# Block-sparse attention into top-1 experts: probabilities as the stationary operand, denominators and gate logits taken from the same matmul, bounds with queries stationary

## The chip, the cores and the metric

The kernel runs on one core of one Trainium2 chip, written in Bass with the Tile scheduler. The metric is the time of one execution on the device in microseconds. The engines are PE (TensorE), DVE (VectorE), ACT (ScalarE), POOL (GpSimd) and SP (SyncE, which here only issues transfers).

## The reference

Attention over 4 batches of 8 heads, 768 tokens, head size 64, in fp32, and then a mixture of 8 experts with one expert per token:

```python
ub = sum(maximum(q * k_min[chunk], q * k_max[chunk]))   # bound per query and chunk of 32 keys
sel = the 6 chunks with the largest ub among the causal ones
scores = q @ k.T / 8, kept where sel and causal, else -1e9
attn = softmax(scores) @ v                               # 3072 tokens x 512
expert = argmax(attn @ w_gate); gate = softmax(attn @ w_gate)[expert]
out = gate * (relu(attn @ w1[expert]) @ w2[expert])      # 512 -> 1024 -> 512
```

## The kernel before

**Pairs.** Two heads make a pair, so there are 16 pairs (`i`), four per batch (`hp` = 0 to 3 within batch `b`). A pair's work is cut into seven units `u` by the causal triangle: a query half `qb` of 384 tokens against key blocks of 128. Units 0 and 1 belong to the first half, 2 to 6 to the second; units 1 and 6 hold two narrower parts (256 and 128 queries).

**Scores (L396 to L420).** Keys are stationary in 64-column tiles (bf16), queries stream. Extra rows of the contraction carry the chunk mask, so a deselected chunk receives -50 before the exponential. ACT takes the exponential from PSUM into a tile P in fp32 (L416); blocks on the diagonal are cut to a triangle by POOL (affine_select, L420).

**Values (`av`, L423).** Values (128 keys x 64) are stationary, P streams, and the output gathers transposed (head dimension on partitions, 384 tokens on columns) in one PSUM accumulator `po`, of which there is one buffer. DVE copies it out (`out_t`, L437) and sums the P tiles of a half into the first of them (`add`, L441), for the softmax denominators.

**Router (`router_steps`, L448 to L515).** `ud` multiplies the P sums by a column of ones and the transposed output by the gate weights, in tiles of 32 columns; ACT copies the result, `lgp_t` and `x_t` transpose it and the output back to tokens on partitions; DVE divides (`lgp`, `xr`), POOL adds the logits over heads. The `ud` of pair i-1 stands inside pair i.

**Bounds.** `k_red` (DVE) takes the minimum and maximum of each chunk, `kse` spreads them into block-diagonal tiles KS (minimum) and KD (maximum less minimum), 64 columns. `ub` (L350) has them stationary and streams the transposed queries qT and their positive part qA; ACT copies, `select_t` transposes, `select` adds the causal bias and takes the sixth largest of 24 per query, `mask` (L379) turns the result and puts it into the extra rows of the query tile QSB. qA of the second query half is made by POOL (`q_r(1)`, L253), which in a pair's order stands behind the triangles of its units 0 and 1.

**Order.** The loop at L883 runs over pairs. PE's, POOL's and DVE's orders are the order of the text; ACT's and the loads' are the scheduler's. In pair i the work on the bounds and mask of pair i+1 and the key and query transposes of pair i+2 lie between the units. Loads go out on SP's queue; POOL issues the expert weights and the scatters.

**Routing and experts.** When a batch's four pairs are done, `logits` makes a one-hot of the winning expert (DVE), `rank` counts tokens with 12 small matmuls, `rank_v` makes each token's slot, and `scatter` (POOL) sends the rows to their slots in HBM. For batch b-1 logits and rank stand in pair hp = 1 of batch b, scatters in hp = 2 and 3. The last batch's are made at the tail (from L978), among the first expert tiles: `up(j)` is the first matrix of token tile j, a transposing transfer makes hT, `down(j)` is the second matrix.

## Time and profile before

| | us |
|---|---|
| median of 9 runs | 359.33 |
| lowest, highest | 357.76, 360.48 |
| the profiled execution | 359.52 |
| its span | 357.8 |
| PE busy | 330.1 |
| POOL, ACT, DVE busy | 241.1, 224.1, 220.7 |
| pair 1's first scores start | 32.45 |
| pairs 2 to 13, from first scores to first scores | 167.84 |
| the first expert matmul starts | 241.78 |

A row of the timeline reads: start in us, time from its first start to its last end, engine, line, operation, output<-inputs, tile, shape, count, and in brackets the engine's idle time before it with what ended it. PEld rows are weight loads. A row by stretch gives the stretch, its length, the busy time and count of PE, PEld, DVE, ACT and POOL in it, the clock, the share of the DMA engines and GB/s. Group rows give busy time, the mean in ns, and the idle time before.

### The profile page before, as it was taken

Reading aid. Unit: us, or ns where it says so; the run is one execution under the profiler, and the core shown is the slowest. Engines: PE = TensorE matmul, PEld = TensorE weight load, DVE = VectorE, ACT = ScalarE, POOL = GpSimd, SP = SyncE. Lnnn points to the kernel's source line nnn. Section 1 sums busy time; section 2 is a strip of 40 time slices with the busy share of each in tenths; the row PEclk is TensorE's granted clock in tenths of the full one; section 3 lists DMA queues with packets and bytes.
Section 4 is the critical chain, followed back from the end, with each engine's and each line's share of the span. In section 5 each row is a group of like instructions: output and inputs, shape, how many; then the busy total and the mean of one; then the engine's idle time right before and its main releaser. Section 6 shows DMA issues by size and latency. Waiting matters only on the chain. (4 is left out here: it accounts for less than half of the span.)

```text
span 357.8 us, 8008 instructions
## 1 busy us (share of the span) xinstructions
PE 330.1 (92%) x2599; PEld 180.4 (50%) x2599; DVE 220.7 (62%) x734; ACT 224.1 (63%) x369; POOL 241.1 (67%) x347
## 2 busy tenths in 40 slices
PE   6779999999999999999999999788789999999980
PEld 3345656556566556565555655344334444444430
DVE  8779788788998878998898999762640000000000
ACT  3487787787787786877867875542334444545430
POOL 7536786695478998659988957877565555655331
PEclk9999999999999999999999999999999999999997
DMA  9999999979457999927997953526799998988950
GB/s 179 214 211 175 231 195 197 187 147 212 91 134 109 238 200 171 187 67 146 193 200 154 179 85 64 116 70 146 173 204 225 223 222 193 215 196 191 190 139 22
DMA packets 138185, 59.86 MB, mean 167 GB/s; under 512 B 122779, under 2 KB 130973, under 8 KB 138144
## 3 DMA queue, kind: packets, MB, share of 16 engines
q0 software_dynamic: 17536, 29.42, 42.9%
q1 hardware_dynamic: 120608, 29.91, 42.8%
q8 instruction: 23, 0.38, 0.4%
q14 instruction: 18, 0.15, 0.1%
HBM read 56.14 MB, written 10.51 MB: 186 GB/s over the span
## 5 line engine op out<-in xcount | busy, mean ns | idle before, releaser
L416 ACT ACTIVATE Pr<-ps 128x768 f32<-128x768 f32 (+2 forms) x112 | 66.7, 628 | 24.9 <-PE ps L411 24.1
L445 DVE TENSOR_TENSOR Pa<-Pa,Pr 128x768 f32<-128x768 f32 (+2 forms) x80 | 68.4, 855 | 7.5 <-PE po L433 2.4
L433 PE MATMUL po<-Pr,v 128*64 128x384 f32 (+2 forms) x448 | 62.8, 400 | 2.3 <-POOL Pr L420 2.0
L420 POOL TENSOR_SCALAR_AFFINE_SELECT Pr<-Pr 128x256 f32<-128x256 f32 x80 | 44.7, 582 | 20.5 <-ACT Pr L416 19.7
L737 PE MATMUL py<-w_all,hT 128*128 x224 | 52.8, 379 | 2.1 <-DMA hT<-h__4950 0.9
L411 PE MATMUL ps<-QSB,KTE 128*64 128x384 bf16 (+2 forms) x576 | 54.2, 293 | 0.3 <-ACT QSB L330 0.2
L411 PEld LDWEIGHTS <-KTE 128*64 128x64 bf16 x576 | 30.1, 109 | 27.1 <-issue 22.1
L433 PEld LDWEIGHTS po<-Pr,v 128*64 128x64 f32 x448 | 29.8, 136 | 23.5 <-issue 10.6
L253 POOL TENSOR_SCALAR qA<-qT 128x384 f32<-128x384 f32 x28 | 38.8, 1384 | 3.8 <-DVE qT L249 3.7
L737 PEld LDWEIGHTS <-hT 128*128 128x128 bf16 x224 | 21.9, 98 | 29.1 <-DMA hT<-h__4950 1.4
L238 ACT ACTIVATE KTE<-pt 64x384 bf16<-64x384 f32 x64 | 31.0, 484 | 3.5 <-DVE kmn L235 2.9
L416 ACT ACTIVATE Pa<-ps 128x768 f32<-128x768 f32 x32 | 25.8, 807 | 10.7 <-PE ps L411 10.7
L721 PE MATMUL ph<-w_all,KTE 128*128 x120 | 28.3, 379 | 1.7 <-issue 0.9
L433 PE MATMUL po<-Pa,v 128*64 128x384 f32 x128 | 26.2, 488 | 1.6 <-POOL Pa L420 1.6
L583 POOL DMA_INDIRECT xs_dram<-xrow,sli x21 | 23.3, 1109 | 6.0 <-issue 4.6
L744 POOL DMA_INDIRECT out_dram<-y,ti x14 | 13.8, 988 | 19.5 <-ACT y L743 19.2
L195 POOL DMA_DIRECT2D w_all<-in_moe_w_dram x32 | 25.6, 802 | 0.2 <-issue 0.2
L721 PE MATMUL ph<-w_all,QSB 128*128 x104 | 24.6, 379 | 0.5 <-issue 0.4
L234 DVE TENSOR_REDUCE kmx<-pt 128x12 f32<-128x384 f32 x32 | 17.6, 551 | 7.2 <-ACT KTE L238 5.8
L513 DVE TENSOR_TENSOR xrow<-xp,rec 128x384 bf16<-128x384 f32 x28 | 15.4, 553 | 9.6 <-PE xp L509 9.5
L256 POOL CAST QSB<-qT 64x384 bf16<-64x384 f32 x32 | 17.0, 552 | 6.0 <-DVE qT L249 3.0
L721 PEld LDWEIGHTS <-KTE 128*128 128x128 bf16 x120 | 11.6, 98 | 15.9 <-issue 2.2
(221 smaller groups left out, 579.1 us busy)
## 6 DMA issues: line engine op xcount, KB each, us to landing
w_all<-in_moe_w_dram POOLq DMA_DIRECT2D x32, 512.0 KB, 7.6
v<-in_v_dram SPq DMA_DIRECT2D x32, 192.0 KB, 5.4
k<-in_k_dram SPq DMA_DIRECT2D x16, 192.0 KB, 4.4
q<-in_q_dram SPq DMA_DIRECT2D x16, 192.0 KB, 4.4
w_all<-in_k_dram SPq DMA_DIRECT2D x16, 192.0 KB, 6.9
w_all<-in_q_dram SPq DMA_DIRECT2D x16, 192.0 KB, 3.8
xs_dram<-xrow,sli POOLq DMA_INDIRECT x21, 4.9
out_dram<-y,ti POOLq DMA_INDIRECT x14, 3.3
```

The lines of the kernel that those rows point to most:

```text
L195: d = nc.gpsimd.dma_start(out=dst, in_=src.rearrange("(c p) f -> p c f", p=128))
L234: nc.vector.tensor_reduce(s["kmx"][:, ts(hf, 12)], v_, AX.X, ALU.max)
L238: nc.scalar.activation(kte[0:64, hd, ts(hf, 384)], s[f"kp{hf}"][64 * hd:64 * hd + 64, :], AF.Copy, bias=0.0, scale=0.125)
L253: nc.gpsimd.tensor_scalar(qA[:], s[f"qT{hf}"][:], 0.0, None, ALU.max)
L411: nc.tensor.matmul(pv[c:c + CW, hd, :], lhsT=kte[:, hd, ds(kb * 128 + c, CW)], rhs=qsb[:, hd, ds(qb * 384 + 384 - w, w)], start=True, stop ...
L416: nc.scalar.activation(P[:, :, ds(c0, w)], pv, AF.Exp)
L420: nc.gpsimd.affine_select(out=pd, in_=pd, pattern=[[0, 2], [1, 128]], compare_op=ALU.is_ge, fill=0.0, base=0, channel_multiplier=-1)
L433: nc.tensor.matmul(s["po"][64 * hd:64 * hd + 64, 384 - w:384], lhsT=vt[:, kb, hd, :], rhs=P[:, hd, ds(c0, w)], start=first, stop=last and ...
L445: nc.vector.tensor_tensor(acc[:, :, 384 - w:384], acc[:, :, 384 - w:384], P[:, :, ds(c0, w)], ALU.add)
L583: d = nc.gpsimd.indirect_dma_start(out=xs_dram[:], out_offset=bass.IndirectOffsetOnAxis(ap=sli[:, u:u + 1], axis=0), in_=bst[b][f"xrow{u % ...
L721: nc.tensor.matmul(ph[:, fh, :], lhsT=xT[:, c, :], rhs=w_all[:, ds(wo + (c * F + fh * 512), 512)], start=(c == 0), stop=(c == NDC - 1), sk ...
L737: nc.tensor.matmul(py[:], lhsT=hT[:, c, :], rhs=w_all[:, ds(wo + (W1W + c * DM), DM)], start=(c == 0), stop=(c == NFC - 1))
```

## The change

P becomes the stationary operand in tiles of 64 queries, and a row of 73 columns streams: 64 values, a column of ones and 8 columns of gate-weighted values. The output then has tokens on partitions, beside the denominators and the gate logits of the head, and `norm` (DVE) divides out of PSUM. The gate-weighted values are made from transposed values (`v_t`, `v_c`, `vw`, `vw_c`) a pair ahead. `ud`, `lgp_t`, `lgp`, `x_t`, `xr`, `out_t`, `add`, `select_t` and the copies ubT and `q_va` are gone. `ub` has qT and qA stationary in 64-column tiles and streams KS and KD of 48 columns; it stands ahead of scores(i, 2), where it stood behind av(i, 1). Logits and rank move to hp = 0, slots and gates to hp = 1, scatters to hp 1 to 3, the two parts of the expert table to pairs 13 and 14. In the last two pairs DVE cuts the triangles. Values are loaded two pairs ahead into three buffers. In pair 0 the steps are ordered anew, and pair 2's qA is made whole there.

```diff
-    DC = 2 * E
     CW = 64
+    VW = D + 1 + E
...
+    V = [buf.tile([128, NT, 2 * VW], FP32, name=f"V{i}") for i in range(3)]
+    nsel = buf.tile([128, NT, 2, 32], BF16, name="nsel")
...
+        for i in range(3):
+            for c in (0, 2 * VW - 1 - E):
+                nc.gpsimd.memset(V[i][:, :, c:c + 1], 1.0)
...
+            t_ = V[i % 3][:, :, 1 + E:1 + E + 2 * D].rearrange("p t (a d) -> p t a d", d=D)
         for hd in range(2):
-            nc.sync.dma_start(out=t_[:, :, hd, :],
+            nc.sync.dma_start(out=t_[:, :, 1 - hd if nm == "v" else hd, :],
...
-        def q_va(hf):
-            qT = s[f"qT{hf}"] = work.tile([128, 384], FP32, tag=f"qT{hf}", name="qT")
-            nc.scalar.activation(qT[:], s[f"qp{hf}"][:], AF.Copy)
...
+        def v_t(hf):
+            pt = ps_m.tile([128, 384], FP32, tag="m")
+            for t in range(3):
+                nc.tensor.transpose(pt[:, ts(t, 128)], V[i % 3][:, 3 * hf + t, 1 + E:1 + E + 2 * D], ident_f[:])
+            s[f"vp{hf}"] = pt
+
+        def v_c(hf, act=False):
+            if hf == 0:
+                s["vT"] = work.tile([128, S], FP32, tag="vT", name="vT")
+            dst = s["vT"][:, ts(hf, 384)]
+            if act:
+                nc.scalar.activation(dst, s[f"vp{hf}"][:], AF.Copy)
+            else:
+                nc.vector.tensor_copy(out=dst, in_=s[f"vp{hf}"][:])
+
+        def vw():
+            pw = s["vwp"] = ps_m.tile([128, NT, 2, E], FP32, tag="m", name="vwp")
+            for kb in range(NT):
+                for c in range(0, 128, CW):
+                    nc.tensor.matmul(pw[c:c + CW, kb].rearrange("p a e -> p (a e)"),
+                                     lhsT=s["vT"][:, ds(kb * 128 + c, CW)], rhs=wgb[:, i % HP, :],
+                                     start=True, stop=True, skip_group_check=True)
+
+        def vw_c():
+            for hd in range(2):
+                c = (2 * VW - E, 1)[hd]
+                nc.vector.tensor_copy(out=V[i % 3][:, :, c:c + E], in_=s["vwp"][:, :, hd])
...
         def ub():
-            pu = ps_m.tile([128, 384], FP32, tag="m")
-            for w_, nm in ((ks, "qT"), (kd, "qA")):
-                for hf in range(2):
-                    nc.tensor.matmul(pu[64 * hf:64 * hf + 64, :], lhsT=w_[:], rhs=s[f"{nm}{hf}"][:],
-                                     start=(nm == "qT"), stop=(nm == "qA"), skip_group_check=True)
-            s["ubT"] = work.tile([128, 384], FP32, tag="qT0", name="ubT")
-            nc.scalar.activation(s["ubT"][:], pu[:], AF.Copy)
+            pu = s["ubp"] = ps_m.tile([128, NT, 2, NCH], FP32, tag="m", name="ubp")
+            for hf in range(2):
+                for t in range(3):
+                    for w_, nm in ((ks, "qT"), (kd, "qA")):
+                        for c in range(0, 128, CW):
+                            nc.tensor.matmul(pu[c:c + CW, 3 * hf + t].rearrange("p a n -> p (a n)"),
+                                             lhsT=s[f"{nm}{hf}"][:, ds(t * 128 + c, CW)], rhs=w_[:],
+                                             start=(nm == "qT"), stop=(nm == "qA"), skip_group_check=True)
+
+        def bound():
+            s["ubm"] = work.tile([128, NT, 2, NCH], FP32, tag="ubm", name="ubm")
+            s["top8"] = work.tile([128, NT, 2, 8], FP32, tag="top8", name="top8")
+            nc.vector.tensor_tensor(s["ubm"][:], s["ubp"][:],
+                                    cbias[:].unsqueeze(2).to_broadcast([128, NT, 2, NCH]), ALU.add)
+
+        def maxes(lo, hi):
+            for t in range(lo, hi):
+                for hd in range(2):
+                    nc.vector.max(out=s["top8"][:, t, hd], in_=s["ubm"][:, t, hd])
+
+        def choose(lo, hi):
+            u3 = s["ubm"][:].rearrange("p t a n -> p (t a) n")[:, 2 * lo:2 * hi]
+            t3 = s["top8"][:].rearrange("p t a n -> p (t a) n")[:, 2 * lo:2 * hi, TOPK - 1:TOPK]
+            nc.vector.tensor_tensor(nsel[:].rearrange("p t a n -> p (t a) n")[:, 2 * lo:2 * hi, 0:NCH], u3,
+                                    t3.to_broadcast([128, 2 * (hi - lo), NCH]), ALU.is_lt)
+
...
+        def put():
+            pt = s["pm"]
+            nc.vector.tensor_copy(out=qsb[64:64 + NCH, 1, :], in_=pt[32:32 + NCH, :])
             nc.scalar.activation(qsb[64:64 + NCH, 0, :], pt[0:NCH, :], AF.Copy)
-            nc.scalar.activation(qsb[64:64 + NCH, 1, :], pt[32:32 + NCH, :], AF.Copy)
...
-        tag, bufs = ("Pa", 3) if u in (0, 2) else ("Pr", 4)
-        P = work.tile([128, 2, 384], FP32, tag=tag, bufs=bufs, name=tag)
+        P = work.tile([128, 2, 384], FP32, tag="P", bufs=6, name="P")
...
+                if i >= NP - 2:
+                    nc.vector.tensor_tensor(pd, pd, tri_b[:].unsqueeze(1).to_broadcast([128, 2, 128]),
+                                            ALU.mult)
+                else:
...
     def av(i, u):
         s = st[i]
         qb, parts = units[u]
-        P, vt = s[f"P{u}"], s["v"]
-        first, last = u in (0, 2), u in (1, 6)
-        if first:
-            s["po"] = ps_o.tile([128, 384], FP32, tag="o", name="po")
-            s[f"acc{qb}"] = P
-        for n, (kb, w, c0) in enumerate(parts):
-            for hd in range(2):
-                nc.tensor.matmul(s["po"][64 * hd:64 * hd + 64, 384 - w:384], lhsT=vt[:, kb, hd, :],
-                                 rhs=P[:, hd, ds(c0, w)], start=first,
-                                 stop=last and n == len(parts) - 1, skip_group_check=True)
-
-    def out_t(i, qb):
-        ot = st[i][f"ot{qb}"] = work.tile([128, 384], FP32, tag="ot", bufs=3, name="ot")
-        nc.vector.tensor_copy(out=ot[:], in_=st[i]["po"][:])
-
-    def add(i, u):
-        qb, parts = units[u]
-        acc, P = st[i][f"acc{qb}"], st[i][f"P{u}"]
-        for n, (kb, w, c0) in enumerate(parts):
-            nc.vector.tensor_tensor(acc[:, :, 384 - w:384], acc[:, :, 384 - w:384],
-                                    P[:, :, ds(c0, w)], ALU.add)
-
-    def router_steps(i):
+        P, vt = s[f"P{u}"], V[i % 3]
+        if u in (0, 2):
+            s[f"po{qb}"] = ps_o.tile([128, 3, 2, D + 2 + 2 * E], FP32, tag="o", name="po")
+        po = s[f"po{qb}"]
+        for kb, w, c0 in parts:
+            for t in range(3 - w // 128, 3):
+                col = c0 + w - 384 + t * 128
+                for hd in range(2):
+                    for c in range(0, 128, CW):
+                        nc.tensor.matmul(po[c:c + CW, t].rearrange("p a d -> p (a d)")[:, ds(hd * VW, VW)],
+                                         lhsT=P[:, hd, ds(col + c, CW)],
+                                         rhs=vt[:, kb, ds((1 - hd) * VW, VW)], start=(kb == 0 and t == 0 and hd == 0), stop=(kb == 3 * qb + t),
+                                         skip_group_check=True)
+
+    def norm(i, hf):
...
+        po = s[f"po{hf}"]
+        ex = po[:, :, 0, D:D + 2 + 2 * E].rearrange("p t (a e) -> p t a e", a=2)
+        rec = work.tile([128, 3, 2], FP32, tag="rec", bufs=2)
+        nc.vector.reciprocal(rec[:], ex[:, :, :, 0])
+        nc.vector.tensor_tensor(
+            bst[b][f"xrow{hf}"][:, :, ts(hp, 128)].rearrange("p t (a d) -> p t a d", d=D),
+            po[:, :, :, 0:D], rec[:].unsqueeze(3).to_broadcast([128, 3, 2, D]), ALU.mult)
+        nc.vector.tensor_tensor(s["lgt"][:, :, hf], ex[:, :, :, 1:1 + E],
+                                rec[:].unsqueeze(3).to_broadcast([128, 3, 2, E]), ALU.mult)
+
+    def lg_add(i):
+        b, hp = divmod(i, HP)
+        eng = nc.vector if i == NP - 1 else nc.gpsimd
+        lg, lgt = bst[b]["lg"], st[i]["lgt"]
+        if hp == 0:
+            eng.tensor_tensor(lg[:], lgt[:, :, :, 0], lgt[:, :, :, 1], ALU.add)
+        else:
             for hd in range(2):
+                eng.tensor_tensor(lg[:], lg[:], lgt[:, :, :, hd], ALU.add)
...
-        todo = {(2, 0): (0,), (2, 1): (2,), (2, 2): (4,), (3, 0): (1,), (3, 1): (3,), (3, 2): (5,)}
+        todo = {(1, 1): (0,), (1, 3): (2,), (2, 1): (4,), (2, 3): (1,), (3, 1): (3,), (3, 3): (5,)}
         if b == B - 1:
-            todo = {(2, 0): (0,), (2, 1): (2, 4), (2, 2): (1,), (2, 3): (3, 5)}
+            todo = {(1, 1): (0,), (1, 2): (2,), (1, 3): (4,), (2, 0): (1,), (2, 1): (3,), (2, 2): (5,)}
...
             b, hp = divmod(i, HP)
-            r = rout[i - 1]
+            pi = prep[i]
             pn = prep[i + 1] if i + 1 < NP else None
-            j = i + 2
-            pj = prep[j] if j < NP else None
+            pj = prep[i + 2] if i + 2 < NP else None
+            rb = route[b - 1] if b > 0 else None
 
             av(i - 1, 6)
-            out_t(i - 1, 1)
-            load(i + 1, "v")
+            pi["vw"]()
+            norm(i - 1, 1)
+            pi["vw_c"]()
+            load(i + 2, "v")
+            lg_add(i - 1)
             scores(i, 0)
             scores(i, 1)
-            if hp == 2 and b > 0:
-                route[b - 1]["rank_v"]()
             if pn:
-                pn["q_r"](1)
+                if i > 1:
+                    pn["q_r"](1)
+                else:
+                    pn["q_s"](0)
                 pn["q_c"](0)
                 pn["q_c"](1)
                 pn["q_d"](1)
-            if hp == 1 and b > 0:
-                route[b - 1]["logits"]()
-            if hp == 2 and b > 0:
-                route[b - 1]["gate"]()
-            if i == NP - 2:
-                begun = table(True)
-                next(begun)
-            if i == NP - 1:
-                next(begun, None)
             weights(4 * i)
             scatters(i, 0)
             early(i, 0)
 
-            def mid():
-                r["ud"]()
-                scores(i, 2)
-
-            keys(j, mid)
+            if pj:
+                pj["k_t"](0)
+                pj["k_t"](1)
+                load(i + 4, "k")
+                pj["k_red"](0)
+                pj["k_out"](1, 0)
+                pj["k_out"](1, 1)
+                pj["k_red"](1)
+                pj["k_out"](0, 0)
+                pj["k_out"](0, 1)
+            if hp == 1 and rb:
+                rb["rank_v"]()
+                rb["gate"]()
+
+            if pn:
+                pn["ub"]()
+            scores(i, 2)
 
             av(i, 0)
             scores(i, 3)
             av(i, 1)
-            add(i, 1)
-            out_t(i, 0)
             if pn:
-                pn["ub"]()
-            if pj:
-                pj["kse"]()
+                pn["bound"]()
+                pn["maxes"](0, 3)
+            norm(i, 0)
+            if pn:
+                pn["maxes"](3, 6)
+                pn["choose"](0, 6)
+            if i == NP - 3:
+                begun = table(True)
+                next(begun)
+            if i == NP - 2:
+                next(begun, None)
             weights(4 * i + 1)
             scatters(i, 1)
             early(i, 1)
 
-            r["lgp_t"]()
-            r["x_t"](0)
-            if pn:
-                pn["select_t"]()
-            r["lgp"]()
-            r["xr"](0)
-            if pn:
-                pn["select"]()
+            if pj:
+                pj["q_t"](0)
+                pj["q_t"](1)
+                load(i + 4, "q")
+                pj["q_v"](0)
+                pj["q_v"](1)
 
             scores(i, 4)
             av(i, 2)
+            scores(i, 5)
             weights(4 * i + 2)
-            scores(i, 5)
+            scatters(i, 2)
+            early(i, 2)
             av(i, 3)
             scores(i, 6)
-            scatters(i, 2)
-            early(i, 2)
-
-            r["x_t"](1)
             if pj:
-                pj["q_t"](0)
-            r["xr"](1)
-            add(i, 3)
-            early(i, 3)
+                pj["q_r"](0)
+                pj["q_s"](0)
+                pj["kse"]()
 
             if pn:
                 pn["mask"]()
-            if pj:
-                pj["q_t"](1)
-                load(i + 4, "q")
+                pn["put"]()
+                pn["v_t"](0)
+                pn["v_t"](1)
+                pn["v_c"](0)
+                pn["v_c"](1)
+            early(i, 3)
+
             av(i, 4)
-            if pj:
-                pj["q_v"](0)
-                pj["q_r"](0)
-                pj["q_s"](0)
-                pj["q_va"](1)
-            add(i, 4)
-            add(i, 5)
+            if hp == 0 and rb:
+                rb["logits"]()
             av(i, 5)
-            if hp == 1 and b > 0:
-                route[b - 1]["rank"]()
+            if hp == 0 and rb:
+                rb["rank"]()
             weights(4 * i + 3)
             scatters(i, 3)
             early(i, 4)
...
-        out_t(NP - 1, 1)
+        norm(NP - 1, 1)
+        lg_add(NP - 1)
...
-            rt["ud"]()
-            rt["lgp_t"]()
-            rt["x_t"](0)
-            rt["x_t"](1)
-            rt["lgp"]()
-            rt["xr"](0)
-            rt["xr"](1)
```

## The prediction

> **What bounds the kernel now.** I read the busy shares first, then the row of 40 slices, then busy time by stretch for each head pair, then TensorE's timeline inside one pair.

> ```profile
> PE 330.1 (92%) x2599; PEld 180.4 (50%) x2599; DVE 220.7 (62%) x734; ACT 224.1 (63%) x369; POOL 241.1 (67%) x347
> PE   6779999999999999999999999788789999999980
> PEclk9999999999999999999999999999999999999997
> ```

> TensorE (PE) is at nine tenths or more nearly everywhere; it dips at the start, near slices 26 to 29 (the hand-over from attention to experts) and at the end. The clock row stays full, so no time is owed to a throttle.

> ```profile
> 60.73:74.42 13.69, 13.69 (x134) 8.34 (x131) 11.67 (x36) 10.84 (x20) 9.86 (x16) 1.00 0.94 167
> 229.36:241.78 12.42, 10.44 (x105) 5.76 (x102) 8.87 (x24) 6.07 (x10) 9.77 (x14) 1.00 0.27 74
> ```

> From one pair's first scores to the next pair's (i=3, a pair without routing) PE is busy 13.69 of 13.69 us; DVE has 2.0 spare, ACT 2.9, POOL 3.8. What is taken off DVE and ACT alone is therefore worth nothing here. The last pair (second line) is different: PE idles 2.0.

> ```profile
> 60.73 0.82 PE L411 MATMUL ps<-QSB,KTE 128*64 128x384 bf16 x12
> 61.48 0.87 PE L226 MATMUL pt<-ident_f,w_all 128*128 128x128 f32 x6
> 62.29 0.85 PE L468 MATMUL pu<-Pa,dcol 128*32 128x384 f32 x8
> ...
> 63.72 0.52 PE L411 MATMUL ps<-QSB,KTE 128*64 128x384 bf16 x4
> 64.07 0.81 PE L433 MATMUL po<-Pa,v 128*64 128x384 f32 x4
> 64.71 0.49 PE L411 MATMUL ps<-QSB,KTE 128*64 128x384 bf16 x4
> 65.04 0.82 PE L433 MATMUL po<-Pr,v 128*64 128x256 f32 x8
> 65.69 0.81 PE L354 MATMUL pu<-qT,KS 128*64 128x384 f32 x4
> 66.33 0.81 PE L354 MATMUL pu<-qA,KD 128*64 128x384 f32 x4
> 67.08 0.55 PE L487 MATMUL lgp<-ident_f,ud 128*128 128x128 f32 x3
> ```

> Starts are to be subtracted here, since ends overlap. One unit of scores is 0.33 (64.71 to 65.04); one unit of values-times-probabilities (av) 0.64 to 0.65, which is four passes over 384 columns, 0.16 a pass or 0.42 ns per column and pass (an fp32 matmul leaves two records, a pass each; two column groups share the time). Six fp32 transposes are about 0.65, three 0.33, or 0.11 each, and a change between 64-column and full-width tiles adds about 0.1 (61.48 to 62.29 is 0.81).

> ```profile
> 134.20 0.87 PE L433 MATMUL po<-Pa,v 128*64 128x384 f32 x4 [0.41 <-POOL Pa L420]
> ```

> This av began after a stall, so its weight load was not hidden: 0.87 in place of 0.81. A pair of 64-column loads costs about 0.06, or 28 ns a pass.

> **The change part by part, PE in a steady pair.** Removed: av 7 x 0.64 = 4.5; the denominator and gate matmuls (L468) 1.43 (62.29 to 63.72); twelve transposes (lgp, both xp, selp) 12 x 0.11 = 1.3; the old bounds 1.28 (65.69 to 66.97). Together 8.5.

> Added: (a) av as 84 matmuls of 73 columns, 168 passes. By streaming, 73 x 0.42 = 31 ns a pass, 5.2 us. That is just above the 28 ns a pass for loads, so I take 31. Bounds: streaming is the floor; the ceiling is the densest long run of matmuls with a load each that the timeline shows, the six mask transposes in about 0.33, 56 ns each, or 9.4 us. I take the floor since it comes from the same tile width and column groups, while those transposes fill the array and stream 128 columns each. (b) Bounds: 24 matmuls of 48 columns, 48 passes; 48 x 0.42 = 20 ns is under the load's 28, so loads set it: 1.35. (c) Gate-weighted values (vw): 12 of 16 columns, 24 passes x 28 ns = 0.7. (d) Six value transposes 0.65. Together 7.9. PE changes between tile widths three times less: -0.3. Balance: 13.69 - 8.5 + 7.9 - 0.3 = 12.8.

> [...]

> **DVE, ACT, POOL.** DVE loses the P sums and gains a copy of the transposed values; ACT loses three PSUM copies. Both had slack in the pair, so nothing: PE covers it, and if PE were no longer the bound they would be shorter anyway.

> ```profile
> L445 DVE TENSOR_TENSOR Pa<-Pa,Pr 128x768 f32<-128x768 f32 x48 | 47.6, 991 | 2.3 <-POOL Pr L420 0.5
> ```

> The output accumulator has one buffer. After the first half's last av, DVE now does three operations on it in place of one copy: 0.23 + 0.55 + 0.26 (reciprocal, xrow, lgt in the rows of before) = 1.04, and about 0.1 of hand-overs. PE has q_t 0.65 and scores 0.33 in between, so 0.15 is exposed (0 to 0.4).

> **The new wait.** The bounds of pair i+1 move ahead of scores(i,2); before, they stood behind av(i,1). Their second half needs relu(q) of the second query half, which POOL makes (q_r(1)) and which stays behind the triangles of units 0 and 1 in POOL's written order:

> ```profile
> 62.20 0.42 POOL L420 TENSOR_SCALAR_AFFINE_SELECT Pa<-Pa 128x256 f32<-128x256 f32 x1
> 62.62 0.76 POOL L420 TENSOR_SCALAR_AFFINE_SELECT Pr<-Pr 128x256 f32<-128x256 f32 x2
> 63.36 1.16 POOL L253 TENSOR_SCALAR qA<-qT 128x384 f32<-128x384 f32 x1
> ```

> The pair began at 60.73, so it is ready at +3.8; the triangles wait for exponentials of this same pair (ACT, 61.26 and 61.97 to 62.84), so it can't come much sooner. Before, PE used it at 66.33, +5.6: hidden. Now PE gets there at 0.75 (two scores) + 0.81 (key transposes) + 0.67 (first half of the bounds) = +2.2. The wait is 1.6 (1.4 to 1.7, as POOL's relu took 0.9 to 1.2 without contention). Scores(i,2) and everything after queue behind it on PE; ACT and POOL get their next exponentials later too. After it: 0.67 + five scores 1.65 + seven av 5.2 + q_t 0.65 + mask 0.33 + v_t 0.65 + vw 0.7 + changes 0.4 = 10.2. So a pair takes 3.85 + 10.2 + 0.15 = 14.2; the balance above, 12.8 + 1.6 + 0.15, gives 14.55. I take 14.3: the wait eats the whole saving and 0.6 more.

> **Pair by pair against the trace.** Pairs 2 to 13 took 167.84 (starts 47.03 to 214.87). Twelve at 14.3 are 171.6. Routing now puts the rank matmuls behind av 5 in pairs 4, 8 and 12; they wait for DVE's one-hot, which follows two value copies:

> ```profile
> 145.82 0.19 DVE L523 TENSOR_REDUCE rmax<-lg 128x6 f32<-128x48 f32 x1
> 147.24 0.56 DVE L534 TENSOR_TENSOR oh<-cand,m 128x48 bf16<-128x48 f32 x1
> ```

> 0.6 for the last copy and 2.0 for these five operations, against 1.5 of PE's two av: 1.1 waited, and 0.4 for the matmuls: +4.5 over three pairs (0.4 each if DVE is early: 1.2). Scatters ahead of the triangles on POOL in pairs 6, 7, 10, 11: +0.8 (0 to 2). Together 176.9, so +9.1.

> The ends gain. Pair 1: 14.58 to 12.8, since its relu was made in pair 0 and the wait is absent: -1.8. Pair 14: POOL's triangles go to DVE, the table part 1 is there: +0.3. Pair 15 to the first expert matmul: 12.42 to 10.2 (seven units of scores and av without preparation, 7 x (0.33 + 0.74) = 7.5, plus vw, the wait for the first exponential and triangle about 2): -2.2. Start: one ACT copy and three transposes leave the chain to the first selection: -0.45 (0 to 1). Hand-over:

> ```profile
> 243.60 0.85 PE L468 MATMUL pu<-Pa,dcol 128*32 128x384 f32 x8
> 250.55 1.89 PE L737 MATMUL py<-w_all,hT 128*128 x8 [0.82 <-DMA hT<-h__3916]
> 254.55 0.20 PE L557 MATMUL pr<-oh,U 128*128 128x48 bf16 x1 [2.12 <-DVE oh L534]
> ```

> Denominators 1.43 and nine transposes 1.0 leave the stretch from 241.78 to 250.55; the transfer of hT then binds, at about 6.3 after the first expert matmul in place of 8.77: -2.4. The 2.1 wait for oh goes, as logits now need only DVE work: -2.2. Sum: 9.1 - 1.8 + 0.3 - 2.2 - 0.45 - 4.6 = +0.35. The profiled execution took 359.52 (span 357.8, 1.7 around it), 0.2 above the median 359.33; so 359.7, rounded 360.

> **DMA and SP.** Value loads go two pairs ahead into three buffers, on the same SP queue with the same bytes: nothing in the steady state (0 to +1; the DMA share of 0.94 at i=3 leaves little spare). On POOL the two logit additions now stand ahead of the triangles and wait for DVE's 1.04 us behind av 6: done before +1.4, where the first triangle starts, so nothing (up to 0.2 a pair if DVE is late); weight and scatter issues stay behind the casts. POOL's new memsets at the start lie beside the first loads: nothing, up to +0.5.

> **Rivals.** A, as above: 360, own range 356 to 366. B, faster: what is left of PE runs at the shorter of my two sums (14.1) and ranks find oh ready: 12 x (14.1 - 14.3) - 3.3 - 0.8, with the hand-over 1.5 better, about 352 (345 to 356). For it: the bottom-up sum contains every row; against: PE lost-time that the rows don't list made the first sum bigger. C, slower: the short matmuls don't reach 31 ns a pass. One nanosecond more costs 168 x 1 ns x 15.5 pairs = 2.6 us; from 31.5 ns on it decides. 37 ns gives 376, and the 56 ns of the mask transposes 425. For it: loads at 28 are just hidden, and PE must take about twice as many instructions per pair; against: twelve rank matmuls with their loads took 0.29 (157.76 to 158.05), 24 ns each. D, the change doesn't do what it says: routing sooner is hidden in any case; in A it is worth only the end's wait.

> **How the numbers follow.** A 0.42, B 0.30, C 0.28. Under 0.3% (1.1 us) this kernel's runs can't tell a change (they spread 357.8 to 360.5). Within A a quarter or so lies inside that, a quarter below, a half above: faster 0.30 + 0.10, same 0.12, slower 0.28 + 0.20. The range 346 to 378 reaches over B nearly whole and into C as far as 38 ns; cases of both signs hold most of it, A's own range is 356 to 366.

> **What would show it.** Pair periods of 14.2 to 14.5; inside, a PE idle of about 1.6 released by POOL's qA at the bounds' second half; av units of 0.74; idle before the rank matmuls in pairs 4, 8, 12; no idle of 2 before the last rank; first down-projection about 6 after the first up. Wrong if av units take over 0.78 (C), or if no idle stands at the bounds.

## The result and the profile after

The changed kernel takes 372.0 us (median of 10 runs, 368.05 to 374.23) against 359.26 for the kernel before (31 runs): 1.033 times as long, 95% interval 1.030 to 1.0355. Its profiled execution took 373.23 with a span of 371.5, so 13.7 more span than before. The forecast was 360, range 346 to 378, with slower the likeliest sign (0.48). Medians are of all executions, ratios of those within 1.5% of their kernel's fastest.

Three lines of the page of the changed kernel (busy time by engine, PE and its clock in 40 slices):

```profile
PE 325.6 (88%) x5319; PEld 243.0 (65%) x5319; DVE 180.2 (49%) x739; ACT 192.0 (52%) x310; POOL 209.9 (56%) x338
PE   6898989889798898978988869888899999999970
PEclk9899999999699999989999998999999999999996
```

DVE, ACT and POOL have all lost work, by 30 to 40 us each. PE has twice as many matmuls, is hardly less busy (325.6 for 330.1), and now has pauses: dips all along the row. New are four dips in the clock row, at slices 2, 11, 18 and 25.

| stretch | before | change forecast | change measured |
|---|---|---|---|
| start to pair 1's first scores | 32.45 | -0.45 | +2.4 |
| pair 1 | 14.58 | -1.8 | -1.3 |
| pairs 2 to 13 | 167.84 | +9.1 | +19.6 |
| pair 14 | 14.49 | +0.3 | -0.5 |
| pair 15 to the first expert matmul | 12.42 | -2.2 | -2.1 |
| from there to the end | 116.0 | -4.6 | -4.4 |

PE inside a pair without routing (timeline; the second half of the bounds is the KD row that waits):

```profile
49.91 0.29 PE L376 MATMUL ubp<-KD,qA 128*64 128x48 f32 x4
50.03 0.29 PE L376 MATMUL ubp<-KS,qT 128*64 128x48 f32 x4
50.15 0.29 PE L376 MATMUL ubp<-KD,qA 128*64 128x48 f32 x4
...
52.11 0.32 PE L376 MATMUL ubp<-KD,qA 128*64 128x48 f32 x4 [1.33 <-POOL qA L259]
...
56.96 0.52 PE L430 MATMUL ps<-QSB,KTE 128*64 128x384 bf16 x4
57.28 0.96 PE L458 MATMUL po<-V,P 128*64 128x73 f32 x24
58.05 0.53 PE L430 MATMUL ps<-QSB,KTE 128*64 128x256 bf16 x8
```

The wait that the forecast named stands where it was expected, 1.33 long in place of 1.6: in this pair, which starts at 48.14, PE gets there at +2.6 for +2.2, and qA is ready at +4.0 for +3.8. Four passes of the bounds take 0.12 (49.91 to 50.03 to 50.15), 29 to 30 ns a pass; one av unit takes 0.77 (57.28 to 58.05), 32 ns a pass. The forecast had 28 and 31.

Busy time by stretch, a pair without routing and a pair hp = 1 (PE, PEld, DVE, ACT, POOL, then the clock, the DMA share and GB/s):

```profile
62.62:77.05 14.43, 13.10 (x306) 11.78 (x305) 8.99 (x36) 8.59 (x15) 8.07 (x15) 1.00 0.99 173
92.57:110.95 18.38, 15.93 (x306) 14.35 (x304) 10.52 (x47) 8.70 (x15) 8.54 (x14) 0.81 0.33 76
```

Plain pairs take 14.44 (forecast 14.3). Pairs hp = 0 take 15.5, 15.5 and 16.8 (forecast 15.8). But the pairs hp = 1 take 18.4, 17.05 and 17.0, and there the forecast had a plain pair: 9.5 us too little, most of its error. With the same 306 matmuls PE is 2.8 busier there, at a granted clock of 0.81. PE's timeline of that pair:

```profile
93.33 0.87 PE L232 MATMUL pt<-ident_f,w_all 128*128 128x128 f32 x6
96.66 0.45 PE L376 MATMUL ubp<-KS,qT 128*64 128x48 f32 x4 [2.45 <-DVE kmn L241]
96.90 0.42 PE L376 MATMUL ubp<-KD,qA 128*64 128x48 f32 x4
97.11 0.42 PE L376 MATMUL ubp<-KS,qT 128*64 128x48 f32 x4
...
101.34 0.85 PE L430 MATMUL ps<-QSB,KTE 128*64 128x384 bf16 x4
...
104.14 0.52 PE L430 MATMUL ps<-QSB,KTE 128*64 128x384 bf16 x4
```

The bounds wait at their first matmul, not at the second half, and for the key minimum, which they don't read. They wait 2.45. After that four passes take 0.21 in place of 0.12 and scores read 0.85 for 0.52, until about 103: the granted clock is 0.50 from 96.18 to 103.00, 6.8 us. DVE's timeline there:

```profile
95.63 0.56 DVE L240 TENSOR_REDUCE kmx<-pt 128x12 f32<-128x384 f32 x1 [0.69 <-ACT KTE L244]
96.10 0.55 DVE L241 TENSOR_REDUCE kmn<-pt 128x12 f32<-128x384 f32 x1
96.57 0.20 DVE L551 TENSOR_TENSOR rk<-pr,base_e 128x48 f32<-128x48 f32 x1
```

The rank counts `pr`, made at the end of the pair before, are read only behind the key reductions. Until then they hold one of the three small PSUM buffers; the two key transposes hold the others.

### The profile page after: what moved, and what is told of

Same layout as the page of the kernel before. It is cut to its first block, busy times and chain, and to the rows that moved or that the text cites. A ratio compares the mean times of both kernels' runs of the same rounds, so it can differ in the third digit from the quotient of the medians.

```text
span 371.5 us, 13394 instructions
## 1 busy us (share of the span) xinstructions
PE 325.6 (88%) x5319; PEld 243.0 (65%) x5319; DVE 180.2 (49%) x739; ACT 192.0 (52%) x310; POOL 209.9 (56%) x338
## 4 chain that ended last, share of the span: by engine, by line
PE 53%; POOL 14%; issue 13%; DVE 7%; DMA 6%; ACT 4%; POOLq 1%; DVEq 0%; ACTq 0%
PE po L458 21%; PE ps L430 10%; PE ubp L376 5%; POOL qA L259 4%; PE ph L702 3%; PE pt L250 3%; POOL out_dram L725 3%; ACT P L435 3%; PE py L718 3%; PE vwp L293 2%; PE pt L277 2%; POOL P L443 2%; PE pt L232 2%; DMA spare<-xs_dram,grow 2%; DMA xg<-xs_dram,grow 2%
## 5 line engine op out<-in xcount | busy, mean ns | idle before, releaser
L435 ACT ACTIVATE P<-ps 128x768 f32<-128x768 f32 x144 | 90.7, 665 | 96.6 <-PE ps L430 96.5
L458 PEld LDWEIGHTS po<-V,P 128*64 128x64 f32 x2688 | 99.6, 139 | 11.7 <-issue 3.1
L458 PE MATMUL po<-V,P 128*64 128x73 f32 x2688 | 104.8, 230 | 1.8 <-DVE lgt L487 1.5
L443 POOL TENSOR_SCALAR_AFFINE_SELECT P<-P 128x256 f32<-128x256 f32 x84 | 32.9, 410 | 64.6 <-ACT P L435 63.6
L376 PE MATMUL ubp<-KD,qA 128*64 128x48 f32 x384 | 27.6, 240 | 12.8 <-POOL qA L259 12.8
L376 PE MATMUL ubp<-KS,qT 128*64 128x48 f32 x384 | 27.5, 240 | 9.4 <-DVE kmn L241 7.4
L376 PEld LDWEIGHTS ubp<-KD,qA 128*64 128x64 f32 x384 | 22.2, 154 | 14.0 <-POOL qA L259 14.0
L376 PEld LDWEIGHTS ubp<-KS,qT 128*64 128x64 f32 x384 | 22.0, 153 | 12.2 <-ACT KTE L244 8.1
L483 DVE RECIPROCAL rec<-po 128x6 f32<-128x6 f32 x32 | 6.3, 196 | 40.6 <-PE po L458 40.6
L725 POOL DMA_INDIRECT out_dram<-V,ti x14 | 13.9, 991 | 20.8 <-ACT V L724 18.3
```

The costliest lines, as they stand in the source:

```text
L376: nc.tensor.matmul(pu[c:c + CW, 3 * hf + t].rearrange("p a n -> p (a n)"), lhsT=s[f"{nm}{hf}"][:, ds(t * 128 + c, CW)], rhs=w_[:], start=( ...
L435: nc.scalar.activation(P[:, :, ds(c0, w)], pv, AF.Exp)
L443: nc.gpsimd.affine_select(out=pd, in_=pd, pattern=[[0, 2], [1, 128]], compare_op=ALU.is_ge, fill=0.0, base=0, channel_multiplier=-1)
L458: nc.tensor.matmul(po[c:c + CW, t].rearrange("p a d -> p (a d)")[:, ds(hd * VW, VW)], lhsT=P[:, hd, ds(col + c, CW)], rhs=vt[:, kb, ds((1 ...
L725: d = nc.gpsimd.indirect_dma_start(out=out[:], out_offset=bass.IndirectOffsetOnAxis(ap=ti[:], axis=0), in_=y, in_offset=None, bounds_check ...
```

## The experiments

The ratio is to the kernel before in the same rounds.

| run | median us | ratio, 95% interval |
|---|---|---|
| slot arithmetic first | 363.7 | 1.013 (1.006 to 1.020) |
| relu sooner | 371.6 | 1.020 (1.010 to 1.030) |
| both | 359.0 | 0.989 (0.983 to 0.996) |
| relu twice | 399.75 | 1.112 (1.107 to 1.117) |
| both, loads spread | 354.2 | 0.985 (0.979 to 0.990) |
| both, routing back | 358.2 | 0.992 (0.987 to 0.997) |
| both, loads spread, rank later | 355.9 | 0.989 (0.983 to 0.995) |
| before, av split | 365.15 | 1.0155 (1.011 to 1.020) |
| slot arithmetic first, bounds back | 368.1 | 1.022 (1.012 to 1.032) |
| both, loads spread, full tiles | 424.5 | 1.180 (1.170 to 1.189) |
| the change, full tiles | 491.3 | 1.367 (1.358 to 1.375) |
| both, loads late | 407.5 (one run) | its pairs 2 to 11 are what counts |

### Slot arithmetic first: what holds the bounds in the pairs hp = 1

```diff
+            if hp == 1 and rb:
+                rb["rank_v"]()
             if pj:
                 pj["k_t"](0)
...
             if hp == 1 and rb:
-                rb["rank_v"]()
                 rb["gate"]()
```

> Only DVE's order in the pairs hp = 1 (i = 5, 9, 13) is changed: the slot arithmetic on the rank counts (rank_v) goes ahead of the two key reductions, where the changed kernel has it behind them. Theory 1 (the rank counts hold one of three PSUM buffers, so the bounds must wait for a buffer of the key transposes, and the 2.45 us idle lowers the clock): the wait there falls from 2.45 to the 1.3 of the other pairs, released by POOL's qA, the clock stays at 1.00 in these stretches, the three pairs fall from 18.4, 17.05 and 17.0 to 14.5 to 15.0, the kernel from 372 to about 363. Theory 2 (the key reductions themselves are late on DVE): they come 1.0 us later still, the wait grows to about 3.4 and the kernel to about 375.

Measured 363.7. The stretch of the same pair (columns as above), and PE's timeline in it:

```profile
92.05:106.48 14.43, 13.13 (x307) 11.77 (x304) 10.33 (x47) 8.70 (x15) 8.52 (x14) 1.00 0.42 97
```

```profile
94.38 0.29 PE L376 MATMUL ubp<-KS,qT 128*64 128x48 f32 x4
95.97 0.32 PE L376 MATMUL ubp<-KD,qA 128*64 128x48 f32 x4 [1.30 <-POOL qA L259]
```

The pair is a plain one, clock full; the other two take 14.44 and 14.53. Together the three fall from 52.4 to 43.4, 9.0 us, of which 3 x 1.15 are the waits and the rest the clock. Theory 1 holds: moving one reader of one PSUM tile on DVE takes it all away, and the key reductions, now later by the five operations put ahead of them, hold nobody.

### Relu sooner, and both

```diff
-                if i > 1:
-                    pn["q_r"](1)
-                else:
+                if i == 1:
                     pn["q_s"](0)
...
                 pj["q_r"](0)
+                pj["q_r"](1)
```

> Only POOL's order: the positive part of the second query half is made directly behind that of the first half, a pair sooner, not behind the triangles of units 0 and 1. Theory 1 (that operation alone holds the bounds back): the 1.33 us idle in PE vanishes in ten pairs and 0.96 in two, pairs of 14.44 become 13.1, kernel about 357. Theory 2 (a wait takes its place: first triangle or exponential, PSUM buffer, or DMA): pairs stay at or above 14.0 and the kernel at 367 to 372.

> Both edits together. Theory 1 for both: pairs at 13.1 to 13.3 with those of hp = 1 at 13.3 to 14, clock full, about 346 to 349, so faster than the kernel before by some 11 us. If either theory 2 holds, 357 or more.

Relu sooner alone gave 371.6, both 359.0. The waits for qA are gone, as theory 1 said, yet the price expected of them isn't paid back: from slot arithmetic first to both it is 5 us by the medians, 9 by the ratios, of 16.7 us of waits. What PE waits for now (table of waits, both edits: total, times, longest):

```profile
PE po L458 <- issue: 4.6, 5, 2.0
PE pr L538 <- DVE oh L515: 2.5, 3, 1.6
PE po L458 <- DVE lgt L487: 1.5, 2, 0.8
PE ps L430 <- issue: 1.5, 1, 1.5
```

and one of them in its timeline:

```profile
62.63 1.75 PE L458 MATMUL po<-V,P 128*64 128x73 f32 x31 [1.98 <-issue]
```

"issue" means that the profile shows nothing that PE waits for. The trace's DMA records show what it is: PE's instructions come in transfers of 16 KB of about 1 us each, 44 of them for 11241 instructions, so 256 in each (before, 23 for 5756). One landed at 61.21, and PE went on 1.42 later; the waits that end at 48.06, 54.23 and 87.41 end 1.36, 1.46 and 1.43 after a landing. Counting the PE instructions begun 1.25 us after the k-th landing (k from 0, its sequencer's instructions included), less 256 k, gives a number that can't pass a certain bound if PE runs dry:

```
kernel                      largest   landings with 448 or more
before                        301       0 of 23
the change                    449       5 of 44
slot arithmetic first         449       3 of 44
both                          449      10 of 44
both, loads spread            453      11 of 44
before, av split              449       1 of 39
both, loads late              448       2 of 44
```

PE stops at the same place of its instruction stream time after time. The 1.33 us waits of the changed kernel gave the supply time to catch up; without them PE comes up against it (10 landings of 44 at the bound in place of 5). The clock takes its part too: behind three waits of this trace (1.98, 1.55 and 1.49 us) it is half for 3.41 us each.

### Relu twice: the clock

```diff
         def q_r(hf, n=1):
...
+            for _ in range(n):
...
-                    pn["q_r"](1)
+                    pn["q_r"](1, 2)
```

> POOL does that positive part twice (the same values again), so the idle before the second half of the bounds grows by 1.16 to about 2.5 us in pairs 2 to 13. If an idle of this length lowers the clock of what follows (theory 1 of the slow hp = 1 pairs): the pairs lose 1.2 and 1.5 to 3 more, clock 0.8 to 0.9 in the stretches, kernel 400 to 420. If the low clock comes from something else in those pairs (the rank matmuls, the scatters): +1.16 in some eleven pairs, 384 to 386, clock 1.00.

Measured 399.75, just under the 400 to 420 that the first case gave. A plain pair (i=3), a part of it and another plain pair (i=6), by stretch, and i=3 in PE's timeline:

```profile
63.43:80.74 17.31, 14.73 (x306) 13.13 (x304) 8.98 (x36) 8.58 (x15) 9.23 (x16) 0.90 0.83 150
69.00:72.42 3.42, 3.42 (x52) 3.01 (x50) 1.07 (x7) 0.81 (x1) 1.70 (x3) 0.50 0.90 168
116.07:131.75 15.68, 13.10 (x307) 11.78 (x304) 8.99 (x36) 8.58 (x15) 11.19 (x20) 1.00 0.80 147
```

```profile
68.59 0.32 PE L377 MATMUL ubp<-KD,qA 128*64 128x48 f32 x4 [2.58 <-POOL qA L260]
68.74 0.29 PE L377 MATMUL ubp<-KS,qT 128*64 128x48 f32 x4
...
71.47 0.86 PE L431 MATMUL ps<-QSB,KTE 128*64 128x384 bf16 x4
...
73.93 0.52 PE L431 MATMUL ps<-QSB,KTE 128*64 128x384 bf16 x4
```

The pair i=3 is 2.87 longer than the 14.44 of the change: 1.25 by the wait, 1.6 since the clock is half from 69.00 to 72.42 and scores take 0.86 for 0.52. No rank matmul or scatter is near, so here the idle time by itself, 2.58, lowers the clock. Its length alone doesn't decide, though: pair 6 has a wait of 2.58 too and keeps its clock, and so does pair 2.

The clock records of the kept traces show why. Half-speed stretches are whole steps of 3.41 us long, and start whole steps apart (the changed kernel's, up to the last matmuls: 10.84 to 14.26, 96.18 to 103.00, 161.03 to 164.44, 222.47 to 225.88). In the twelve traces with 64-column tiles, from the first matmul on, a step in which PE was idle for 1.81 us or more was always followed by one at half speed, and one with 1.31 or less never was, unless it ran at half speed itself; between the two both happened. A wait that straddles two steps is divided: 2.57 in pair 2 into 1.60 and 0.98, 2.58 in pair 6 into 1.55 and 1.03, 2.08 in the run with loads spread into 0.50 and 1.58, all without loss of clock, where 2.05 at the start of the changed kernel lay in one step and was followed by half speed.

### Loads spread, loads late: why instructions come late

```diff
-    slots = [4 * i + g for i in range(NP - 2) for g in range(4) if i < HP or i % HP != 1]
+    slots = [4 * i + g for i in range(NP - 2) for g in range(4)]           # loads spread
+    slots = [4 * i + g for i in (NP - 4, NP - 3) for g in range(4)]        # loads late
```

> On top of both edits of the run with the slot arithmetic first and the relu sooner: the expert weight loads are spread over all 56 slots of pairs 0 to 13, hp = 1 pairs too, in place of 44, so that the stretches with a full DMA share carry fewer bytes. Theory 3 (PE now starves for instructions: its waits for nothing the profile shows end 1.4 us after a 16 KB instruction transfer, which comes late where DMA is full): those waits (some 8 us with the low clock behind them) shrink by half or more, kernel 350 to 355. Theory 4 (the instruction supply is slow by itself, whatever the DMA share): the same waits, 356 to 360.

354.2, within the range, but the waits without releaser did not shrink: 7.2 us in pairs 2 to 11, and 11 landings at the bound. So the time doesn't decide, and the reason given was not supported by it. The loads are levelled, not fewer.

> On top of slot arithmetic first and relu sooner: 26 of the 32 expert weight loads are issued in pairs 12 and 13, so that pairs 2 to 11 run with no load but their own keys, queries and values; the end will be late and isn't asked about. With the loads spread these ten pairs took 140.6 (48.12 to 188.72), with 7.2 us of waits that have no releaser. Theory 3 (16 KB instruction transfers come late behind the other DMA work): those waits fall under 2 us and the ten pairs take 131 to 134. Theory 4 (the supply is too slow by itself at some 600 PE instructions a pair): the waits stay at 5 to 9 us and the ten pairs at 138 to 143.

Busy time from 48 to 180, first with loads spread, then with loads late, each from its own trace:

```profile
48.00:180.00 132.00, 125.03 (x2858) 112.23 (x2858) 88.50 (x362) 82.06 (x146) 84.93 (x149) 1.00 0.89 165
```

```profile
48.00:180.00 132.00, 130.21 (x3016) 117.30 (x3016) 92.94 (x379) 85.52 (x152) 76.93 (x140) 1.00 0.44 103
```

With the DMA share at 0.44 (one execution) the ten pairs take 132.8 (47.20 to 179.98) in place of 140.6, no wait without releaser is left in them, and a plain pair is 12.89 with PE busy all of it. Theory 3 holds: the supply of some 600 PE instructions a pair suffices at a DMA share of 0.44, and comes late behind the loads at 0.89. In these 132 us the 16 KB transfers themselves take about as long in both runs (median 0.97 with loads spread, 1.11 with loads late), so it is probably their start that is late.

### Before, av split: instructions by themselves

```diff
-            for hd in range(2):
-                nc.tensor.matmul(s["po"][64 * hd:64 * hd + 64, 384 - w:384], lhsT=vt[:, kb, hd, :],
-                                 rhs=P[:, hd, ds(c0, w)], start=first,
+            for x in range(0, w, 64):
+                for hd in range(2):
+                    nc.tensor.matmul(s["po"][64 * hd:64 * hd + 64, ds(384 - w + x, 64)], lhsT=vt[:, kb, hd, :],
+                                     rhs=P[:, hd, ds(c0 + x, 64)], start=first,
```

> The kernel before with one edit: av streams P in pieces of 64 columns (36 records a pair become 168 to 170), the same columns and sums. Streaming 64 x 0.42 = 27 ns a pass stands against 28 for a load, so about +0.1 to 0.2 a pair or 2 to 3 us by that alone: 361 to 363. Theory 3 or 4 (instruction supply): PE had no pause in its pairs, so waits that the profile gives no releaser appear in the pairs of full DMA, with a lower clock behind the longer of them: 365 to 375. Without such waits the supply isn't the limit.

Every piece of a half's first unit opens the accumulation anew, and this kernel's output, unlike what was expected, leaves out part of the sums, probably of that unit; count and size of the instructions are as said. A plain pair, by stretch:

```profile
60.85:74.90 14.05, 14.05 (x268) 10.88 (x266) 11.65 (x36) 10.84 (x20) 9.84 (x16) 1.00 0.95 168
```

365.15, but for another reason than the supply: the pairs grow by 0.37 each, 132 more passes at some 3 ns more, and have next to no waits without releaser (one of 0.3 in all). 268 matmuls in 14.05 us are still supplied, with one landing at the bound. So the theory's expectation for this run failed: twice the instructions are not enough by themselves; at 306 in 13.1 us, and a full DMA, they were.

### Bounds back behind av(i,1)

```diff
-            if pn:
-                pn["ub"]()
             scores(i, 2)
 
             av(i, 0)
             scores(i, 3)
             av(i, 1)
             if pn:
+                pn["ub"]()
                 pn["bound"]()
```

> On top of the slot arithmetic moved first (that run gave 363.7): the bounds go back behind av(i,1), where the kernel before has them; POOL's order stays. If their new place is what makes the wait, PE reaches their second half at +4.4 or later, after qA (+3.8): the 1.33 us waits vanish and the kernel falls as with the relu made sooner, to 356 to 360 (less than the 16 us of the waits, since PE then meets waits without a releaser). If something else held PE, it stays at 362 to 365.

A miss: 368.1, no faster than the 363.7 without this edit (the intervals of the two ratios overlap). The waits for qA are gone, but PE's timeline shows a new one:

```profile
73.11 0.31 PE L458 MATMUL po<-V,P 128*64 128x73 f32 x3 [0.84 <-DVE lgt L487]
```

and DVE's timeline why:

```profile
71.06 0.46 DVE L383 TENSOR_TENSOR ubm<-ubp,cbias 128x288 f32<-128x288 f32 x1 [1.36 <-PE ubp L376]
71.55 0.61 DVE L389 MAX8 top<-ubm 128x8 f32<-128x24 f32 x6
72.08 0.18 DVE L483 RECIPROCAL rec<-po 128x6 f32<-128x6 f32 x1
```

`bound` and three of the six maxima stand ahead of `norm` on DVE. With later bounds `norm` is late, and with it the one output accumulator: 0.84 in nearly every pair (12.7 us in 14 waits). A plain pair takes 13.95 in place of 14.44: the wait of 1.33 is traded for one of 0.84. Pairs 1 and 2 (15.0 and 16.2, for 13.3 and 14.5) have waits without releaser. Pairs 2 to 13 together take 176.0 in this trace and 177.2 without the edit, so the steady state isn't slower. Of the 4.7 us by which the profiled span is longer (364.2 for 359.5), 4.0 lie behind the first expert matmul, where the first down-projection waits 3.36 for its transfer of hT in place of 1.27, with a step of half speed behind it; why that transfer came late was not followed up. What the run shows of the order is this: with the bounds back, DVE's order holds PE where POOL's did.

### Routing back, rank later

```diff
-            if hp == 0 and rb:
-                rb["rank"]()
+            if hp == 1 and rb:
+                rb["rank"]()                       # routing back; logits, slots, scatters, table likewise
```

> On top of both edits: logits, rank, slots, gates, scatters, table and first gathers where the kernel before has them, one pair later. If routing sooner is worth nothing in the steady state: the wait for the one-hot (0.5 to 1.5) moves from pairs 4, 8, 12 to 5, 9, 13 and the kernel stays at 356 to 361. If the earlier gathers shorten the hand-over to the experts, it is 2 to 4 us slower, 361 to 364.

358.2 against 359.0 with the same edits: the intervals of the two ratios overlap nearly whole. Routing a pair sooner is worth nothing that these runs can tell.

```diff
             scores(i, 2)
+            if hp == 1 and rb:
+                rb["rank"]()
+                rb["rank_v"]()
```

> Loads spread, and the rank matmuls moved from the end of the hp = 0 pairs to behind the third scores of the hp = 1 pairs, where the one-hot is long done; the slot arithmetic follows them on DVE. The three waits of 0.5 to 1.6 vanish and no PSUM buffer is held at the bounds: 2 to 4 us less than with the loads spread alone, 347 to 352. If starving takes the time back: the same as with the loads spread alone.

The waits for the one-hot are gone from the trace, but rank waits 0.6 three times for a PSUM buffer that ACT's key copies release, and 355.9 is no better than 354.2: the waits without releaser still come to 7.4 us in pairs 2 to 11. Inconclusive as to the 1.6 us at stake.

### Full tiles: what two column groups are worth

```diff
-    CW = 64
+    CW = 128
```

> On top of slot arithmetic first, relu sooner and loads spread (that run gave 354.2): the stationary tiles of scores, values, bounds and gate-weighted values are 128 columns wide in place of two of 64 (one constant). The same streaming, half the instructions, and no changes between tile widths inside a pair. If a 128-column fp32 load (about 2 x 28 = 57 ns by the pair of loads) hides under a pass of 73 x 0.84 = 61 ns: 10 or more changes of 0.1 go and the waits without releaser too, pairs of 12 to 12.5 and 338 to 346. If the load isn't hidden under a pass that uses the same rows and columns, av grows by up to 5 us a pair: 375 to 430.

> The changed kernel with that constant alone. Waits at the bounds stay (2.45 in hp = 1 pairs with the lower clock behind it, about 1.3 to 1.6 elsewhere). If full tiles are good: 358 to 366. If the loads aren't hidden: above 385.

424.5 and 491.3. PE's timeline of the first:

```profile
81.30 1.46 PE L458 MATMUL po<-V,P 128*128 128x73 f32 x12
82.59 0.49 PE L430 MATMUL ps<-QSB,KTE 128*128 128x384 bf16 x2
...
94.01 1.46 PE L293 MATMUL vwp<-wgb,vT 128*128 128x16 f32 x12
95.31 0.82 PE L430 MATMUL ps<-QSB,KTE 128*128 128x384 bf16 x6
```

Twelve passes of 73 columns take 1.29, and twelve of 16 columns take 1.30: 108 ns a pass whatever streams. So the load alone sets it, and the streaming (61 ns by the estimate of the expectation) lies wholly under it, on the same rows and columns. The slow side came, but not for the reason expected: the load of 128 columns is not 57 ns and hidden, but the longer of the two. Two 64-column loads side by side cost 56 to 57 ns (the 24 passes of `vwp` in 64-column tiles take 0.67, 61.95 to 62.62 in the changed kernel: 28 a pass), one of 128 columns 108. Of the further 67 us of the second kernel 12 are waits at the bounds; its clock is lower (0.877 of a span of 490.2, against 0.991 of 420.2), an estimated 56 us if the time lost is the share of the span that the clock lacks. Why waits of 0.93 are enough to lower it there is open.

## Why the prediction was right or wrong

- **The new wait**: right in place and cause, 1.33 for 1.6. The 0.9 for POOL's relu, on which its range of 1.4 to 1.7 rests, is shown by no run: before, it took 1.16 to 1.80 (median 1.22), the nine of 1.79 and more beside one of DVE's sums (`add`); after, 1.15 to 1.25. Doubling the relu and making it sooner both act on it as foreseen.
- **The price of a pair**: 14.44 for 14.3. PE is busy 13.1 of it, and 12.89 in the run with loads late, where it waits for next to nothing: the balance (12.8) was near, the sum of the rows (12.4, without the waits) 0.5 too low. av passes at 32 ns for 31 make 0.2 of that, the rest isn't itemised. The term for the accumulator (0.15) was too much in plain pairs: no wait; it appears as 0.77 in pairs 14 and 15.
- **Pairs hp = 0**: the wait for the one-hot is 0.48, not 1.1; the pairs cost +1.1 for +1.5, and pair 12 more through a wait without releaser of 1.36.
- **Pairs hp = 1: wrong, 9.5 us.** The step that failed is "Twelve at 14.3 are 171.6". It priced routing in pairs 4, 8 and 12 only. It did not follow `rank_v`, which the change puts behind the key reductions, to the PSUM buffer that it releases; and every wait was priced at its length, since "no time is owed to a throttle" was read off the trace of a kernel whose longest waits behind the start (1.99 and 2.12) happened to leave the clock alone: no step of 3.41 us holds more than 1.59 us of idle there.
- **The start: wrong, 2.9 us.** The first scores come 1.0 later and pair 0 is 1.5 longer. That "one ACT copy and three transposes leave the chain" was priced; the wait of 2.05 ahead of the first bounds, with half speed behind it, and the new value transposes, which wait 0.8 for a PSUM buffer that ACT's mask copy releases, were not. The half speed belongs to this one execution: with slot arithmetic first, whose start is the same, the wait is 1.60, the clock stays full and the first scores come at 16.12, not 16.68.
- **The ends**: right. Pair 15 -2.1 for -2.2; the hand-over -4.4 for -4.6, with the first down-projection 6.8 after the first expert matmul (forecast 6.3) and no idle ahead of the last rank.
- **Rivals**: C came out in time, not in mechanism: the short matmuls do run at 31 to 32 ns. That 372.0 lies in the range is in part luck: the range was drawn up to 378 for slow matmuls, and waits filled it. Its doubt about twice the instructions was right in another way, as supply. D is right: routing sooner is worth nothing measurable. B isn't met by the change: its pairs of 14.1 stand against 14.44, and the shorter sum that it goes by, 12.4 without the waits, against 12.89.

## What to carry to other kernels

When a step moves, look at what it releases as well as at what it waits for: here a PSUM tile read some 3 us later by DVE cost 9.0 us, as much as the whole steady state was forecast to lose (9.1). A wait on PE can be paid twice, by its length and by a lower clock behind it: here 2.45 of wait, and half speed for 6.8. And a matmul cut into many small ones needs its instructions brought in: taking away 16.7 us of waits gave 5 to 9, and ten pairs that took 140.6 at a DMA share of 0.89 took 132.8 at 0.44. The change with its two orders mended and the loads spread is 1.5% faster than the kernel before (0.985, 0.979 to 0.990).
